# One value product per head, and the division by the row sums moved behind it, in a fused attention and gated-MoE kernel

## The chip, the cores and the metric

The kernel runs on one core of one Trainium2 chip. The metric is device time in microseconds (us) from the first to the last instruction with what lies around it, of one launch; lower is better. The core has TensorE (matmuls; its weight loads are a row of their own, PEld), VectorE (DVE), ScalarE (ACT), GpSimd (POOL) and SyncE (SP), which here issues nearly all transfers.

## The reference

Attention in which a query sees only the keys that fall into its own bucket of a hash, followed by a feed-forward block with a convolution gate. Shapes: batch 4, 8 heads, 768 positions, 64 per head; the feed-forward block is 512 wide. All is float32.

```
mask = bucket(q @ proj)[:, :, :, None] == bucket(k @ proj)[:, :, None, :]   # 6 bits, 64 buckets
scores = where(mask, q @ k.T / sqrt(64), -1e9)
attn = exp(scores - max(scores))
attn = attn / (sum(attn) + 1e-09)
x = concat_heads(attn @ v)                                    # (4, 768, 512)
gate = sigmoid(sum_k conv_w[k] * x shifted by 4 - k)          # 5 taps, causal, per channel
out = (gate * (x @ w_val)) @ w_out
```

## The kernel before, in words

The work is a stream of 32 units (one head of one batch each), and a unit is six tiles of 128 queries. The main loop (line 453) makes one pass per tile, 192 in all; I call such a pass a slot. Everything is issued in program order: `manual_schedule` (line 442) keeps TensorE, ScalarE, VectorE and GpSimd in the order in which the loop calls the helpers. So the order of the calls in the loop is the order on each engine's queue, and an instruction that waits holds all that stand behind it on its engine. SP's queue is not among those engines.

For tile k the stages lie in several slots:
- `scores(k + 1)` (line 225): four matmuls into one of two PSUM tiles `s`. The mask is inside the product: twelve more rows of the operands hold the hash bits, so that keys of other buckets come out hugely negative.
- `maxima`, `factors`, `shifts` (lines 235 to 248) on VectorE: the row maximum from PSUM and two tiny instructions that make scale and bias of the exponential. They depend on each other.
- `exponentials(k)` (line 250) on ScalarE: p = exp(scale * s + bias), with the row sum as a by-product in `sm`.
- `row_sums`, `recip`, `normalise` (lines 260 to 271): for two tiles at a time the reciprocal of the row sum on VectorE, then p times it on GpSimd, for each tile, two slots after its exponential.
- `transposes(k - LAG)` (line 273) with LAG = 3: six 128x128 transposes on TensorE into two PSUM tiles `tp`, at the end of the slot; `keep_transposed` (line 283) copies them to SBUF on ScalarE at the start of the next slot.
- `attn_v` (line 294): the value product, 24 matmul instructions per unit (6 key blocks, two column halves of the array side by side, each product two instructions), into the PSUM tile `av`. It is a generator; the loop steps it twice in every odd slot, 8 instructions each time. At its end ScalarE copies the result to x (line 311).

The rest is generators that the loop steps once or more per slot: `prep` (line 157) builds a coming head's operands, with a cast of the raw q and k on VectorE, the remainder on GpSimd, and seven transfers on SP, all in one step; `bits` (line 186) makes the hash bits of four heads, with a 32-column matmul into a side tile; `pair_x` (line 317) splits x of two heads into a rounded part (VectorE) and a remainder (GpSimd) and runs the five convolution taps on VectorE; after the fourth pair of a batch come the sigmoids, and `cur["gates"]` is 2 for the next two slots, in which the MoE takes three steps; `moe` (line 350) is the feed-forward block in chunks of three steps (four matmuls each) into one PSUM tile from the pool `ps_m`, which has one buffer. `val` ends with the product with the gate, `ht` (line 370), and later its split (`hh`, `hl`); `outp` ends with a copy of the output tile (ScalarE, or VectorE while gates is set, line 394) and its store. `hold` (line 408) keeps two output chunks back until the next batch's MoE begins. `load_weights` splits the weights during the first heads, mostly on VectorE. After the loop (line 490) the MoE has five PSUM tiles and runs alone.

Of the kernel before, what the change touches and what calls it, by code (L numbers as in the profile page):

```python
# [26 lines left out]
def kernel(  # L27
# [18 lines left out]
    LAG = 3  # L46
# [8 lines left out]
    pp = ctx.enter_context(tc.tile_pool(name="pp", bufs=LAG + 1))  # L55
# [7 lines left out]
    op = ctx.enter_context(tc.tile_pool(name="op", bufs=2))  # L63

# [92 lines left out]
    def prep(i):  # L157
# [8 lines left out]
        nc.vector.tensor_copy(out=aq, in_=r)  # L166
# [10 lines left out]
        if j == 3 and i + 1 < len(units):  # L177
            yield
            yield from bits(i + 1)

    def side_tile():
        if not moes:
            return ps_m.tile([P, 512], FP32, name="m")
        return ps_t.tile([P, 512], FP32, name="tp")

    def bits(i):

        u = stk.tile([P, S], FP32R, name="u", bufs=2)
        for hf in range(2):
            yield  # L190
            sl = slice(hf * HS, (hf + 1) * HS)
            z = side_tile()
            for jj in range(4):
# [3 lines left out]
            nc.vector.tensor_scalar(out=u[:, sl], in0=z[:, 0:HS], scalar1=rows_sb[:, 0:1], scalar2=rows_sb[:, 1:2],  # L197
                                    op0=ALU.is_ge, op1=ALU.mult)
        cur["u"] = u

    def first_bits():
        yield from bits(0)
        load_raw(5)
# [46 lines left out]
    def exponentials(k):  # L250
        s, nb = ss.pop(k), nbs.pop(k)
        p = pp.tile([P, 2, HS], FP32, name="p")
        if k % 2 == 0:
            cur["sm"] = small.tile([P, 2, 2], FP32, name="sm")
        sm = cur["sm"]
        nc.scalar.activation(out=p, in_=s[:, :, 0:HS], func=AF.Exp, bias=nb, scale=gs.pop(k), accum_out=sm[:, k % 2, 0:1])  # L256
        ps[k] = (p.rearrange("p a b -> p (a b)"), sm)


    def row_sums(k):  # L260
        sums[k] = small.tile([P, 2, 2], FP32, name="s1")
        nc.vector.tensor_scalar(out=sums[k][:, :, 0], in0=ps[k][1][:, :, 0], scalar1=1e-9, scalar2=None, op0=ALU.add)

    def recip(k):
        ri = small.tile([P, 2], FP32, name="ri")
        nc.vector.reciprocal(out=ri, in_=sums.pop(k)[:, :, 0])
        rcs[k], rcs[k + 1] = ri[:, 0:1], ri[:, 1:2]

    def normalise(k):
        p, _ = ps[k]  # L270
        nc.gpsimd.tensor_scalar(out=p, in0=p, scalar1=rcs.pop(k), scalar2=1.0, op0=ALU.mult, op1=ALU.mult)  # L271

    def transposes(k):
        p, _ = ps.pop(k)
# [19 lines left out]
    def attn_v(i, pts):  # L294
# [4 lines left out]
        for kb in range(KB):  # L299
            if kb:  # L300
                yield
            for s, pt in enumerate(pts):
                nc.tensor.matmul(out=av[s * D:(s + 1) * D, 0:HS], lhsT=vt[:, kb, hh * D:(hh + 1) * D], rhs=pt[kb // 3][:, kb % 3, :],  # L303
                                 start=(kb == 0), stop=(kb == KB - 1), tile_position=(0, s * D))
        if hh == 0:
            x = cur["x"] = xp.tile([P, S + KW - 1], FP32, name="x")
            nc.gpsimd.memset(x[:, 0:KW - 1], 0.0)
        x = cur["x"]
        for s in range(2):
            o = KW - 1 + s * HS  # L310
            nc.scalar.copy(out=x[hh * D:(hh + 1) * D, o:o + HS], in_=av[s * D:(s + 1) * D, 0:HS])  # L311
        if hh == 1:
            if c == 0:
                cur["xs"], cur["g"] = {}, []
            convs.append(pair_x(b, c, x, cur["g"], cur["xs"]))

    def pair_x(b, c, x, gs, xs_):
        for o in (0, HS):
# [4 lines left out]
            nc.vector.tensor_copy(out=xh, in_=x0)  # L323
            nc.gpsimd.tensor_tensor(out=xl, in0=x0, in1=xh.bitcast(FP32), op=ALU.subtract)  # L324
        yield
# [9 lines left out]
        if c == NP - 1:  # L335
# [3 lines left out]
            cur["gates"] = 2  # L339
            moes.append(moe(b, xs_, gs))  # L340

    def acc_tile():
        pools = accs
# [6 lines left out]
    def moe(b, xs_, g):  # L350
# [3 lines left out]
        def later():  # L354
            while todo:
                todo.pop(0)()

        def val(o, j):
# [11 lines left out]
            nc.vector.tensor_tensor(out=ht, in0=acc[:, 0:HS], in1=g[j][:, o:o + HS], op=ALU.mult)  # L370

            def split():
                hh = hp.tile([P, HS], FP32R, name="hh")
                nc.vector.tensor_copy(out=hh, in_=ht)  # L374
# [6 lines left out]
        def outp(o, tb):  # L381
# [4 lines left out]
            for hi, wi in ((0, 0), (0, 1), (1, 0)):  # L386
# [6 lines left out]
                later()  # L393
            ob = op.tile([P, 512], FP32, name="o")
# [4 lines left out]
            r0 = o + tb * P  # L399
# [157 lines left out]
```

## Time and profile before

| | us |
|---|---|
| median of 3 runs | 638.9 |
| lowest, highest | 638.37, 640.07 |
| the profiled execution's own time | 637.56 |
| its span, first to last instruction | 635.6 |
| VectorE busy | 465.9 |
| ScalarE busy | 421.7 |
| GpSimd busy, of which normalise (L271) | 364.7, 220.0 |

The profiled execution's time and its span differ by 2 us, the start and end of the launch. The granted TensorE clock was 0.989 of full speed on average.

How to read the rows: a group's row gives line, engine and operation, what is written and read, the number of instructions, then after the bar their busy time in us and the mean of one in ns, then the idle time of the engine just before them and what ended it. A timeline row gives start in us, duration in us, then the same names; records of one kind that follow each other are merged (x8), and a bracket tells idle time before. Matmuls are pipelined, so their records overlap, and the distance of two starts is the better measure. A row of waits gives total us, times, and the longest. L12 is line 12 of the kernel before, until a kernel after is spoken of.

### The profile page before, as it was taken

The numbers are of one execution on the slowest core, as the hardware profiler recorded it, in microseconds if no ns is written. First come the engines' busy times: TensorE is split into PE (matmuls) and PEld (weight loads), VectorE is DVE, ScalarE is ACT, GpSimd is POOL, SyncE is SP. The second block draws the span as 40 slices with busy tenths as digits, with TensorE's granted clock in tenths as the row PEclk, the third lists the DMA queues.
The fourth block names the chain that finished last, engine by engine and source line by source line (L and its number), as shares of the span: only waits on it lengthen the run. The fifth ranks groups of instructions, "written<-read, shape, count | busy, mean of one in ns | idle before, by whom it ended". The sixth has DMA issues, their size and how long they took to land.

```text
span 635.6 us, 10630 instructions
## 1 busy us (share of the span) xinstructions
PE 590.1 (93%) x3496; PEld 424.3 (67%) x3496; DVE 465.9 (73%) x1064; ACT 421.7 (66%) x881; POOL 364.7 (57%) x326
## 2 busy tenths in 40 slices
PE   4689888878999999999999999999999999999997
PEld 2465554555567777676667877677667777776895
DVE  5789897999986766668675877578685787665532
ACT  3487776767778666667787766677778677675400
POOL 1375868577765764567653776466562677544221
PEclk9899998998999999999999999999999999999999
DMA  6533535443332334343433333343422223300111
GB/s 243 128 101 86 139 96 138 112 134 81 104 80 58 83 75 123 82 105 96 104 80 79 88 80 110 80 121 80 120 57 61 57 53 79 86 18 2 50 51 50
DMA packets 23269, 56.76 MB, mean 89 GB/s; under 512 B 4296, under 2 KB 4296, under 8 KB 23216
## 3 DMA queue, kind: packets, MB, share of 16 engines
q1 hardware_dynamic: 23072, 56.06, 32.9%
q8 instruction: 28, 0.46, 0.3%
q14 instruction: 25, 0.20, 0.1%
q10 hardware_dynamic: 144, 0.03, 0.0%
HBM read 23.12 MB, written 6.29 MB: 46 GB/s over the span
## 4 chain that ended last, share of the span: by engine, by line
PE 64%; DVE 18%; ACT 10%; issue 3%; DMA 3%; POOL 0%; DVEq 0%; ACTq 0%
PE av L303 16%; PE s L232 15%; PE tp L280 12%; PE m L390 8%; PE m L365 7%; DVE nm L238 6%; ACT p L256 4%; DVE g L334 3%; ACT pt L289 3%; ACT x L311 2%; DMA w<-in_w_out_dram 2%; DVE aq L166 1%; PE tp L365 1%; PE tp L390 1%; PE s L390 1%
## 5 line engine op out<-in xcount | busy, mean ns | idle before, releaser
L271 POOL TENSOR_SCALAR p<-p,ri 128x768 f32<-128x768 f32 x192 | 220.0, 1150 | 200.3 <-DVE nb L248 157.6
L256 ACT ACTIVATE p<-s,nb,gs 128x768 f32<-128x768 f32 x192 | 192.7, 1004 | 49.7 <-DVE nb L248 44.6
L289 ACT COPY pt<-tp 128x384 f32<-128x384 f32 x384 | 166.2, 485 | 86.0 <-PE tp L280 85.0
L238 DVE TENSOR_REDUCE nm<-s 128x1 f32<-128x768 f32 x192 | 182.4, 950 | 52.8 <-PE s L232 52.6
L280 PEld LDWEIGHTS tp<-ident,p 128*128 128x128 f32 x1152 | 130.4, 142 | 74.2 <-issue 47.3
L280 PE MATMUL tp<-ident,p 128*128 128x128 f32 x1152 | 165.4, 280 | 4.5 <-ACT pt L289 1.6
L232 PE MATMUL s<-ak,aq 76*128 76x384 f32 x384 | 118.6, 390 | 32.2 <-ACT p L256 25.4
L303 PE MATMUL av<-pt,vt 128*64 128x384 f32 x768 | 146.9, 504 | 0.0
L232 PE MATMUL s<-bk,bq 128*128 128x384 f32 x384 | 101.6, 346 | 0.0
L232 PEld LDWEIGHTS s<-ak,aq 76*128 76x128 f32 x384 | 59.4, 195 | 48.9 <-ACT p L256 39.3
L303 PEld LDWEIGHTS av<-pt,vt 128*64 128x64 f32 x768 | 47.4, 137 | 63.3 <-issue 62.7
L334 DVE SCALAR_TENSOR_TENSOR g<-x,cw_sb,g 128x768 f32<-128x768 f32 x64 | 78.4, 1225 | 0.2
L232 PEld LDWEIGHTS s<-bk,bq 128*128 128x128 f32 x384 | 71.9, 194 | 0.5 <-issue 0.5
L376 POOL TENSOR_TENSOR hl<-ht,hh 128x384 fp32r<-128x384 f32 x32 | 33.4, 1044 | 45.5 <-DVE hh L374 45.5
L168 POOL TENSOR_TENSOR bq<-r,aq 128x768 fp32r<-128x768 f32 x31 | 58.4, 1885 | 0.5 <-DVE aq L166 0.5
L311 ACT COPY x<-av 64x384 f32<-64x384 f32 x64 | 30.4, 475 | 33.5 <-PE av L303 32.9
L365 PE MATMUL m<-xh,wv 128*128 128x384 f32 x200 | 42.7, 337 | 0.0
L248 DVE TENSOR_SCALAR nb<-nm,gs 128x1 f32<-128x1 f32 x192 | 40.1, 209 | 3.5
L370 DVE TENSOR_TENSOR ht<-m,g 128x384 f32<-128x384 f32 x25 | 13.9, 555 | 35.4 <-PE m L365 32.0
L256 ACT ACTIVATION_READ_ACCUMULATOR p<-s,nb,gs 128x1 f32 x192 | 39.1, 204 | 0.0
L324 POOL TENSOR_TENSOR xl<-x,xh 128x384 fp32r<-128x384 f32 x32 | 33.5, 1066 | 9.5 <-DVE xh L323 9.5
L390 PE MATMUL m<-wo,hh 128*128 128x512 f32 x144 | 38.1, 394 | 0.0
(84 smaller groups left out, 475.6 us busy)
## 6 DMA issues: line engine op xcount, KB each, us to landing
r<-in_qk_dram SPq DMA_DIRECT2D x32, 384.0 KB
vt<-in_v_dram SPq DMA_DIRECT2D x16, 384.0 KB
out_dram<-o SPq DMA_DIRECT2D x24, 256.0 KB
ak<-aq SPq DMA_DIRECT2D x31, 192.0 KB
bk<-aq SPq DMA_DIRECT2D x31, 192.0 KB
bk<-bq SPq DMA_DIRECT2D x31, 192.0 KB
bq<-aq SPq DMA_DIRECT2D x31, 192.0 KB
w<-in_w_val_dram SPq DMA_DIRECT2D x4, 512.0 KB
```

What stands on the lines that cost most here:

```text
L168: nc.gpsimd.tensor_tensor(out=bq, in0=r, in1=aq.bitcast(FP32), op=ALU.subtract)
L232: nc.tensor.matmul(out=s[:, hf, 0:HS], lhsT=lq[0:n, qs], rhs=rk[0:n, hf * HS:(hf + 1) * HS], start=n == M, stop=n == P)
L238: nc.vector.tensor_reduce(out=nm, in_=s[:, :, 0:HS], axis=AX.XY, op=ALU.max, negate=True)
L256: nc.scalar.activation(out=p, in_=s[:, :, 0:HS], func=AF.Exp, bias=nb, scale=gs.pop(k), accum_out=sm[:, k % 2, 0:1])
L271: nc.gpsimd.tensor_scalar(out=p, in0=p, scalar1=rcs.pop(k), scalar2=1.0, op0=ALU.mult, op1=ALU.mult)
L280: nc.tensor.transpose(out=tp[:, n * P:(n + 1) * P], in_=p[:, kb * P:(kb + 1) * P], identity=ident)
L289: nc.scalar.copy(out=pt[:, :, qo:qo + P], in_=tp[:, 0:HS].rearrange("p (a b) -> p a b", b=P))
L303: nc.tensor.matmul(out=av[s * D:(s + 1) * D, 0:HS], lhsT=vt[:, kb, hh * D:(hh + 1) * D], rhs=pt[kb // 3][:, kb % 3, :], start=(kb == 0), s ...
L311: nc.scalar.copy(out=x[hh * D:(hh + 1) * D, o:o + HS], in_=av[s * D:(s + 1) * D, 0:HS])
L334: nc.vector.scalar_tensor_tensor(out=g, in0=x[:, k:k + S], scalar=w, in1=g, op0=ALU.mult, op1=ALU.add)
L365: nc.tensor.matmul(out=acc[:, 0:HS], lhsT=wv[wi][:, c, j * P:(j + 1) * P], rhs=xs_[(c, o)][xi], start=(m == 0), stop=(m == 11))
L390: nc.tensor.matmul(out=acc, lhsT=hs[(o, j)][hi][:, tb * P:(tb + 1) * P], rhs=wo[wi][:, j, :], start=(m == 0), stop=(m == 11))
```

## The change

It changes eight things.

1. The value product of a unit is issued whole, in the slot r = 1 of the next unit (`finish(avs)`; r is the slot's place in its unit, 0 to 5). No MoE step is taken in that slot; slot r = 4 takes a second one after its transposes.
2. p is no longer normalised. The row sums of the six tiles of a unit lie in one tile; at r = 0 VectorE takes their reciprocals once per unit, SP writes them to memory, and at r = 1 SP reads them back, spread over 64 partitions twice (`rb`). At r = 3 `take` forms x from `av` on VectorE, as a product with `rb`, whose factors it reads at every third element.
3. LAG is 1: a tile's transposes come one slot after its exponential.
4. Casts move from VectorE to GpSimd: q and k in `prep`, x in `pair_x`, `ht` in the MoE.
5. `prep` begins at r = 5 and spreads its transfers over r = 0, 2 and 3. At the start two steps are taken per slot.
6. The hash bits use the PSUM tile of the value product, at r = 4 and 5.
7. Instructions that read a PSUM tile are put off to the next slot: the bits' comparison and `ht` (list `late`, behind the maximum), and the copy of the output tile with its store (list `puts`, behind the exponential).
8. The convolution takes four steps at r = 2 and one at r = 1; in a batch's last pair and at the end one per slot.

```
@@ prep
-        nc.vector.tensor_copy(out=aq, in_=r)
+        nc.gpsimd.tensor_copy(out=aq, in_=r)
         yield
         nc.gpsimd.tensor_tensor(out=bq, in0=r, in1=aq.bitcast(FP32), op=ALU.subtract)
         nc.sync.dma_start(out=ak[0:D].bitcast(FP32), in_=aq[D:P].bitcast(FP32))
         nc.sync.dma_start(out=bk[0:D].bitcast(FP32), in_=aq[D:P].bitcast(FP32))
+        yield
+        yield
         nc.sync.dma_start(out=bk[D:P].bitcast(FP32), in_=bq[D:P].bitcast(FP32))
+        yield
         nc.sync.dma_start(out=bq[D:P].bitcast(FP32), in_=aq[0:D].bitcast(FP32))
...
@@ bits
-            z = side_tile()
+            z = pool.tile([P, 512], FP32, name=name)
...
-            nc.vector.tensor_scalar(out=u[:, sl], ...
+            late.append(lambda z=z, sl=sl: nc.vector.tensor_scalar(
...
+    def row_sums(i):
+        s1 = small.tile([P, KB], FP32, name="s1", bufs=2)
+        nc.vector.tensor_scalar(out=s1, in0=sms.pop(i), scalar1=1e-9, scalar2=None, op0=ALU.add)
+        ri = small.tile([P, KB], FP32, name="ri", bufs=2)
+        nc.vector.reciprocal(out=ri, in_=s1)
+        rows = dp.tile([2, P, KB // 2], FP32, name="rows")
+        nc.sync.dma_start(out=rows.rearrange("s p t -> p s t"), in_=ri.rearrange("p (s t) -> p s t", s=2))
+        return rows
+
+    def row_factors(i, rows):
+        rb = rbs[i] = rp.tile([P, P, KB // 2], FP32, name="rb")
+        for s in range(2):
+            nc.sync.dma_start(out=rb[s * D:(s + 1) * D], in_=rows[s].partition_broadcast(D))
...
+    def take(i, av):
...
         for s in range(2):
             o = KW - 1 + s * HS
-            nc.scalar.copy(out=x[hh * D:(hh + 1) * D, o:o + HS], in_=av[s * D:(s + 1) * D, 0:HS])
+            nc.vector.tensor_tensor(out=x[hh * D:(hh + 1) * D, o:o + HS].rearrange("d (t p) -> d t p", p=P),
+                                    in0=av[s * D:(s + 1) * D, 0:HS].rearrange("d (t p) -> d t p", p=P),
+                                    in1=rb[s * D:(s + 1) * D].rearrange("d p t -> d t p"), op=ALU.mult)
...
@@ pair_x
-            nc.vector.tensor_copy(out=xh, in_=x0)
+            nc.gpsimd.tensor_copy(out=xh, in_=x0)
             nc.gpsimd.tensor_tensor(out=xl, in0=x0, in1=xh.bitcast(FP32), op=ALU.subtract)
-        yield
...
     def acc_tile():
+        drain(late)
+        drain(puts)
...
@@ val
-            nc.vector.tensor_tensor(out=ht, in0=acc[:, 0:HS], in1=g[j][:, o:o + HS], op=ALU.mult)
+            late.append(lambda: nc.vector.tensor_tensor(out=ht, in0=acc[:, 0:HS], in1=g[j][:, o:o + HS], op=ALU.mult))
...
@@ outp
+            puts.append(lambda: put(o + tb * P, acc))
+            yield
+
+        def put(r0, acc):
             ob = op.tile([P, 512], FP32, name="o")
             if cur["gates"]:
                 nc.vector.tensor_copy(out=ob, in_=acc)
             else:
                 nc.scalar.copy(out=ob, in_=acc)
             nc.sync.dma_start(out=out[b, r0:r0 + P, :], in_=ob)
...
@@ the loop
+            r = k % KB
             if 0 <= k - LAG - 1:
                 keep_transposed(k - LAG - 1)
...
                 maxima(k)
                 factors(k)
                 shifts(k)
+            drain(late)
+            if r == 0 and k:
+                rows = row_sums(tiles[k - 1][0])
+            if r == 1 and k > 1:
+                row_factors(tiles[k - 2][0], rows)
             if k + 1 < N:
...
                 scores(k + 1)
             if k < N:
                 exponentials(k)
-            if k >= 60 or k % 2:
+            drain(puts)
+            whole = bool(avs)
+            for _ in range(1 if whole or k >= N - 10 else 4 if r == 2 else cur["last"]):
                 step(convs)
+            if r == 3:
+                drain(taken)
...
-            for _ in range(3 if cur["gates"] else 1):
+            for _ in range(0 if whole else 3 if cur["gates"] else 1):
                 step(moes)
             cur["gates"] = max(0, cur["gates"] - 1)
             step(preps)
-            if k % 2:
-                step(avs)
-                step(avs)
+            if k < 5:
+                step(preps)
+            if r == KB - 1:
+                finish(preps)
+                preps = [prep(k // KB + 2)]
+                step(preps)
+            finish(avs)
             if 0 <= k - LAG < N:
                 transposes(k - LAG)
+            if r == 4 and not cur["gates"]:
+                step(moes)
```

More of the change, by code (lines that the diff above doesn't have):

```diff
@@ L45 @@
     KW = 5
-    LAG = 3
+    LAG = 1
     scale = 1.0 / float(D) ** 0.5
@@ L178, in prep, with bits @@
             yield
[L179 to L186, printed above, removed]
+            yield from bits(i + 1, ps_v, "av")
+    def bits(i, pool, name):
         u = stk.tile([P, S], FP32R, name="u", bufs=2)
         for hf in range(2):
-            yield
+            if hf:
+                yield
+            drain(late)
             sl = slice(hf * HS, (hf + 1) * HS)
-            z = side_tile()
+            z = pool.tile([P, 512], FP32, name=name)
             for jj in range(4):
@@ L252, in exponentials @@
         p = pp.tile([P, 2, HS], FP32, name="p")
[L253 to L271, printed above, removed]
+        i, qt = tiles[k]
+        if qt == 0:
+            sms[i] = small.tile([P, KB], FP32, name="sm", bufs=2)
+        sm = sms[i]
+        nc.scalar.activation(out=p, in_=s[:, :, 0:HS], func=AF.Exp, bias=nb, scale=gs.pop(k), accum_out=sm[:, qt:qt + 1])
+        ps[k] = p.rearrange("p a b -> p (a b)")
+    def row_sums(i):
[10 more added lines that the diff above has]
+            nc.sync.dma_start(out=rb[s * D:(s + 1) * D], in_=rows[s].partition_broadcast(D))
     def transposes(k):
-        p, _ = ps.pop(k)
+        p = ps.pop(k)
         tps[k] = []
@@ L304, in attn_v @@
                                  start=(kb == 0), stop=(kb == KB - 1), tile_position=(0, s * D))
+        taken.append(lambda: take(i, av))
+    def take(i, av):
+        b, h = units[i]
+        hh, c = h % 2, h // 2
         if hh == 0:
@@ L338, in pair_x @@
                 nc.scalar.activation(out=g, in_=g, func=AF.Sigmoid)
-            cur["gates"] = 2
+            cur["gates"], cur["last"] = 2, False
             moes.append(moe(b, xs_, gs))
     def acc_tile():
+        drain(late)
+        drain(puts)
         pools = accs
@@ L354, in later @@
         def later():
-            while todo:
-                todo.pop(0)()
+            drain(late)
+            drain(todo)
         def val(o, j):
@@ L438, in finish @@
             step(gens)
-    cur["gates"], cur["end"], cur["pts"] = 0, False, []
+    cur["gates"], cur["end"], cur["pts"], cur["last"] = 0, False, [], False
     N = len(tiles)
@@ L496 @@
             step(moes)
-        finish(moes)
+            drain(late)
+            drain(puts)
+        while moes:
+            step(moes)
+            drain(late)
+            drain(puts)
 _INS = ['qk', 'v', 'proj', 'w_val', 'conv_w', 'w_out']
```

42 lines of the change are left out of this document (19 added, 23 removed).

## The prediction

> **What bounds the kernel now.** I read the page's head first, then a table of two windows, then the timeline of TensorE alone, then a stretch of all engines, then the waits.
>
> ```profile
> span 635.6 us, 10630 instructions
> ...
> PE 590.1 (93%) x3496; PEld 424.3 (67%) x3496; DVE 465.9 (73%) x1064; ACT 421.7 (66%) x881; POOL 364.7 (57%) x326
> ```
>
> TensorE is busy 93% of the span, but an average hides stages, so the windows come next.
>
> ```profile
> core 0: us, PE busy (x) PEld busy (x) DVE busy (x) ACT busy (x) POOL busy (x), PEclk, DMA share, GB/s
> 0.00:165.80 165.80, 134.25 (x774) 87.94 (x775) 143.01 (x317) 111.65 (x237) 102.81 (x94) 0.96 0.44 121
> 165.80:635.60 469.80, 455.82 (x2724) 336.34 (x2722) 322.86 (x748) 310.09 (x644) 261.92 (x233) 1.00 0.30 78
> ```
>
> Up to 165.8 us (nine heads; the weights are still being split) VectorE is the busiest, 143 of 165.8 us. Afterwards TensorE is busy 456 of 470 us: whatever shortens TensorE's list there shortens the kernel, and whatever makes it wait is added. So the change has to be priced on TensorE's queue, slot by slot. I call a slot one pass of the main loop (one tile of 128 queries, six per head, r = 0 to 5), S its four score matmuls, T its six transposes, M one step of the MoE (four matmuls). Steady slots:
>
> ```profile
> 415.11 0.86 PE L365 MATMUL m<-xh,wv 128*128 128x384 f32 x4
> 415.90 1.51 PE L303 MATMUL av<-pt,vt 128*64 128x384 f32 x8
> 417.34 0.88 PE L280 MATMUL tp<-ident,p 128*128 128x128 f32 x6
> 417.98 0.59 PE L232 MATMUL s<-ak,aq 76*128 76x384 f32 x2
> ...
> 418.77 0.86 PE L365 MATMUL m<-xh,wv 128*128 128x384 f32 x4
> 419.47 0.82 PE L280 MATMUL tp<-ident,p 128*128 128x128 f32 x6
> 420.04 0.60 PE L232 MATMUL s<-ak,aq 76*128 76x384 f32 x2
> ```
>
> Starts give true pitches, since records overlap. S takes 0.79 (417.98 to 418.77), M of the value projection 0.70, T 0.57 (419.47 to 420.04): 2.06 us for a slot without a value product, with no gap. In a slot with one, M takes 0.79, the eight av matmuls 1.44, T 0.64: the group costs 1.44 + 0.09 + 0.07 = 1.60.
>
> **The change, part by part.**
>
> *1. One value product of 24 matmuls at r = 1 in place of three of 8.* How long is a run of 24? The last head has one already, after the loop:
>
> ```profile
> 585.04 4.39 PE L303 MATMUL av<-pt,vt 128*64 128x384 f32 x24
> 589.36 2.11 PE L390 MATMUL m<-wo,hh 128*128 128x512 f32 x8
> ```
> ```profile
> 585.72 0.15 PEld L303 LDWEIGHTS av<-pt,vt 128*64 128x64 f32 x2 [0.17 <-issue]
> ...
> 588.30 0.15 PEld L303 LDWEIGHTS av<-pt,vt 128*64 128x64 f32 x2 [0.17 <-issue]
> ```
> ```profile
> L256 ACT ACTIVATE p<-s,nb,gs x192: 991/1006/1042, 13.0 to 577.2; 128x768 f32<-128x768 f32 x192
> ```
> ```profile
> 165.80:577.20 411.40, 103.19 (x548) 33.23 (x550) 1.00 0.32 83
> ```
>
> Inside it the pairs follow at (588.30 - 585.72) / 8 = 0.322 us. A group of four pairs is 1.29, so 0.31 of the 1.60 is the price of going into and out of this shape. Twelve pairs in one run: 3.87 + 0.31 = 4.18 against 3 x 1.60 = 4.80, 0.62 saved per head. The run above took 4.32, because its second half started late behind a copy; if each head has that hitch, 0.32 is saved. From 165.8 us to the last exponential 548 av matmuls run (last row), 22.8 heads: **-14.1 us** (bounds -7.3, and -19.2 if the early heads gain too). In front of it stand S and the copies of the transposes, which are done by then, so I take the full value.
>
> *2. The copy of an output tile (`put`) moves from the slot of its last matmul into the next slot, behind that slot's exponential.* This adds a wait: the MoE has one PSUM tile (`ps_m`, one buffer), so the next M cannot start before the copy is done, and T and the next S stand behind that M on TensorE. ScalarE's pace:
>
> ```profile
> 316.68 0.88 PE L280 MATMUL tp<-ident,p 128*128 128x128 f32 x6
> ...
> 317.26 0.86 ACT L289 COPY pt<-tp 128x384 f32<-128x384 f32 x2 [1.23 <-PE tp L280]
> 317.31 0.60 PE L232 MATMUL s<-ak,aq 76*128 76x384 f32 x2
> ...
> 318.01 1.00 ACT L256 ACTIVATE p<-s,nb,gs 128x768 f32<-128x768 f32 x1
> ...
> 318.30 0.96 DVE L238 TENSOR_REDUCE nm<-s 128x1 f32<-128x768 f32 x1 [1.02 <-PE s L232]
> ...
> 318.99 0.87 ACT L289 COPY pt<-tp 128x384 f32<-128x384 f32 x2
> 319.16 0.62 PE L232 MATMUL s<-ak,aq 76*128 76x384 f32 x2 [0.24 <-ACT p L256]
> ...
> 319.61 1.01 DVE L334 SCALAR_TENSOR_TENSOR g<-x,cw_sb,g 128x768 f32<-128x768 f32 x1
> ```
> ```profile
> L370 DVE TENSOR_TENSOR ht<-m,g 128x384 f32<-128x384 f32 x25 | 13.9, 555 | 35.4 <-PE m L365 32.0 <-ACT g L338 3.4
> ...
> L398 ACT COPY o<-m 128x512 f32<-128x512 f32 x12 | 7.0, 587 | 3.2 <-PE m L390 2.2
> ```
>
> From T's start the two copies of T begin after 0.58 (316.68 to 317.26), the exponential 0.75 later, the next ScalarE instruction 0.98 after that: the output copy starts 2.31 us after T and is done at 2.90. T follows the finished M at once; TensorE is back for the next M after T and S, 0.57 + 0.79 = 1.36. It waits 1.54 us with nothing behind to fill in. By the diff's step counts two MoE chunks end per head, at r = 3 and r = 5, and the next chunk begins in the next slot with an M, never with the value product between. Such ends, with ScalarE copying and another chunk right behind: the three tiles of the first half in each of the batches 0 to 2, and the very last tile of batches 0 and 1, behind which the next batch begins. (The first tile of the second half is followed by `hold`, the second is copied by VectorE while `gates` is set, and after the loop there are five PSUM tiles and no deferral.) 11 x 1.54 = **+16.9 us**. If the copy slips in earlier it is 0; it cannot gain, since today's copy holds nobody (M to T has no gap above).
>
> *3. The product with the gate (`ht`) is deferred too, and VectorE gains the division.* From S's start the maximum begins 0.99 later (317.31 to 318.30) and VectorE is free again 1.31 after that (319.61); `ht` takes 0.555, done at 2.86 after S. TensorE's next M is due at 2.06 + 0.79 = 2.85: no wait. But at r = 3 two divisions of 64x384 come first; nearest row `ht`, also one PSUM and one SBUF operand, 0.555 each. The previous maximum's chain ends at -2.06 + 0.99 + 1.31 = 0.24, plus 1.11 is 1.35 instead of 0.99, so M waits 0.37. Nine chunk ends: **+3.3 us** (0 if the division is as fast as its 64 partitions could suggest and fits the gap; see the third rival for the other side).
>
> *4. Slots without an M.* While the MoE holds, TensorE has 1.36 per slot and ScalarE needs 1.73 (317.26 to 318.99), and S waits (0.24 in the row at 319.16). Today every second such slot has a value product, which covers ScalarE; afterwards they come five in a row. Some four more uncovered slots per batch, three batches: 12 x 0.37 = **+4.4 us** (0 to +9).
>
> *5. Waits that go.* With `ht` behind the maximum, exponentials are no longer late, and the side tile of the hash bits no longer takes a transpose's buffer.
>
> ```profile
> PE s L232 <- ACT p L256: 5.1, 15, 0.9
> ...
> PE tp L280 <- DVE u L197: 1.6, 4, 0.4
> ```
>
> **-6.7 us** (0 if all stay).
>
> *6. The first 165.8 us, on VectorE.* Eight heads of it:
>
> ```profile
> L334 DVE SCALAR_TENSOR_TENSOR g<-x,cw_sb,g 128x768 f32<-128x768 f32 x10 | 13.0, 1303 | 0.0
> ...
> L166 DVE CAST aq<-r 128x768 fp32r<-128x768 f32 x8 | 6.0, 755 | 0.0
> ...
> L262 DVE TENSOR_SCALAR s<-sm 128x2 f32<-128x2 f32 x24 | 4.5, 189 | 0.7 <-ACT p L256 0.7
> L266 DVE RECIPROCAL ri<-s 128x2 f32<-128x2 f32 x24 | 4.0, 166 | 0.0
> ...
> L323 DVE CAST xh<-x 128x384 fp32r<-128x384 f32 x6 | 2.6, 471 | 0.0
> ```
>
> Away go the casts, 6.0 + 2.6. In come 16 divisions, 8.9. The row sums look like 8.5 us saved, but they stand today between instructions that wait for each other (maximum, factor, shift), where they cost nothing; once per head at the end of that chain they cost 0.355, 2.8 in all. GpSimd loses the normalisation:
>
> ```profile
> L271 POOL TENSOR_SCALAR p<-p,ri 128x768 f32<-128x768 f32 x192 | 220.0, 1150 | 200.3 <-DVE nb L248 157.6
> ```
>
> With 220 of GpSimd's 365 us gone, the convolution's 1.303 may fall to the 1.01 of the row at 319.61: -2.9. Sum +0.2, **taken as 0**; four convolution steps bunched at r = 2 leave VectorE idle in heads that have none (up to +6), an earlier second `prep` and a quieter GpSimd may give as much.
>
> *The rest costs nothing as long as its cover holds.* GpSimd takes three casts where it gave up 192 normalisations. Scores of the next head need SP's last transfers, issued at r = 3 for r = 5, two slots (4.1 us) ahead. The sums' way through memory:
>
> ```profile
> 40.95 2.29 DMA ak<-u
> ```
> ```profile
> SPq L175 <- PE s L232: 70.7, 15, 7.1
> ```
>
> Two trips of about 2.29 (nearest row) are 4.6 us; between r = 0 and the division at r = 3 lie 1.36 + 5.54 + 2.06 = 9.0. Cover 4.4.
>
> **Sum:** -14.1 + 16.9 + 3.3 + 4.4 - 6.7 + 0 = +3.8. The profiled execution took 637.56 us (span 635.6), so 641.4; the median of the runs shown, 638.9, lies 1.3 above it, so on that scale 642.7: **643 us**. About 0.3% is what a measurement of this kernel can tell from no change.
>
> **The rivals.**
>
> *Faster: the deferred copies hold nobody.* Without the 16.9 of part 2: 626 us. For it: ScalarE is busy only 66%, and a copy that gets in before the exponential in most slots would do. Against: ScalarE works in order, and the copies of T cannot begin before T. It decides from the point where the copy ends within 1.36 of T's start.
>
> *No change: the early part pays.* If VectorE's first 165.8 us are shorter by 5 (quiet GpSimd, earlier second head), 638 us. For it: the 1.303 against 1.01. Against: the bunched convolution.
>
> *Slower: the division is slow.* It reads the factors at every third element. At twice 0.555 it adds 1.11 per head where VectorE paces or delays `ht`: nine early heads and nine chunk ends, +20, 663 us. No row here reads at such a step. [...]
>
> *Slower: the factors come late.* SP works in order; today it stood behind the tiles of `ak` 15 times, 7.1 us at the longest. Past the cover of 4.4 VectorE stops at r = 3 with the next maximum behind it: 15 x 2.7 = 40, 683 us at worst. The transfer that stood there now comes at r = 3, behind these, which speaks against it.
>
> **How the numbers follow.** Forecast 0.46 (with the spread of its terms some of it ends within 0.3% or faster), copies free 0.30, early part pays 0.13, slow division 0.07, late factors 0.04. Faster: 0.30, plus 0.03 of the forecast and 0.03 of the second rival, 0.36. Same: 0.06 of the second rival and 0.07 of the forecast, 0.13. Slower: 0.51. Range 622 to 655: from the first rival with a little more than 14.1 saved, up to the forecast with parts 4 to 6 at their bad ends; the two slow rivals and some of the fringe are left out. The likeliest sign's own range is 641 to 655.
>
> **What would show it.** Right: av in runs of 24 with 4.2 us from start to T; TensorE idle before an M of L365 or L390, released by the output copy on ScalarE, eleven times, some 1.5 us each; ACT and DVE waits of 0.4 at r = 4; VectorE's division near 0.55; its wait for the factors absent. Wrong: no such idle time before M (first rival); a first stage that ends well before 165 us; a division over 0.8 us; VectorE idle until a DMA at r = 3.

## The result: 4.8% slower, and where the time came from

| us | before | after |
|---|---|---|
| median | 638.96 | 669.9 |
| profiled execution, span | 637.56, 635.6 | 671.35, 669.6 |
| heads 1 to 8 | 134.1 | 148.6 |
| heads 9 to 31, to the last exponential | 411.4 | 440.4 |
| TensorE's clock at half in heads 1 to 8; 9 to 31 | 6.8; 0 | 27.3; 10.2 |

The ratio is 1.0476, 95% interval 1.0419 to 1.0534. A stage of heads is counted from the start of its first exponential to the start of the next stage's; the last row adds up the stretches of half speed in the trace's record of TensorE's granted clock, each counted where it begins. A stage's time is that of one profiled execution per kernel, and in the changed kernels the first of heads 1 to 8 alone takes 15.6 to 19.0 us, so two or three us between two stages are no finding. In the fences of this section L12 is a line of the kernel after.

First the page's head and the two windows, cut where the tenth head's first exponential starts (165.8 us before, 178.0 here); their columns are those of the table shown for before.

```profile
span 669.6 us, 10067 instructions
...
PE 588.1 (88%) x3496; PEld 441.0 (66%) x3496; DVE 448.2 (67%) x902; ACT 390.3 (58%) x820; POOL 208.8 (31%) x229
```
```profile
0.00:178.00 178.00, 137.19 (x795) 96.34 (x796) 136.56 (x282) 105.40 (x227) 61.10 (x62) 0.91 0.48 124
178.00:669.60 491.60, 450.95 (x2703) 344.69 (x2701) 311.62 (x621) 284.87 (x593) 147.70 (x168) 0.99 0.34 84
```

Every engine is busy for less time than before (GpSimd 209 us in place of 365), and the kernel is slower: 12.2 us come from the first window, 21.8 from the second. (The 21.8 are 29.0 more up to the last exponential, as in the table, and 7.2 less behind it, 51.2 for 58.4, where 192 matmuls of the MoE are left in place of 212.) In the second TensorE, which sets the time there, is no longer busy 97% but 92%. What it waits for there (total us, times, longest):

```profile
PE s L236 <- ACT p L261: 8.7, 20, 1.7
PE m L407 <- ACT o L419: 8.7, 6, 1.8
PE m L382 <- ACT o L419: 6.6, 5, 1.4
PE m L382 <- DVE ht L387: 6.6, 9, 1.0
PE s L236 <- POOL xl L340: 2.5, 2, 1.3
PE tp L287 <- ACT pt L296: 1.3, 1, 1.3
PE s L236 <- issue: 1.1, 1, 1.1
PE tp L407 <- POOL hh L391: 0.6, 1, 0.6
```
And in the same stage of the kernel before, by its own lines:
```profile
PE s L232 <- ACT p L256: 5.8, 16, 0.9
PE tp L280 <- DVE u L197: 1.6, 4, 0.4
PE tp L280 <- ACT pt L289: 1.0, 2, 0.8
PE s L390 <- DVE hh L374: 0.4, 1, 0.4
```

36.1 us of waits against 8.8, so 27.3 more. Rows two and three are the deferred output copy, row four the deferred product with the gate. The timeline of one deferred copy shows the chain, and something that no row of waits counts:

```profile
231.80 0.81 PE L287 MATMUL tp<-ident,p 128*128 128x128 f32 x6
...
232.80 0.52 PE L236 MATMUL s<-bk,bq 128*128 128x384 f32 x2
...
233.47 0.99 ACT L261 ACTIVATE p<-s,nb,gs 128x768 f32<-128x768 f32 x1 [0.29 <-DVE nb L252]
...
234.45 0.57 ACT L419 COPY o<-m 128x512 f32<-128x512 f32 x1
235.08 1.86 PE L407 MATMUL m<-wo,hh 128*128 128x512 f32 x4 [1.76 <-ACT o L419]
236.73 1.48 PE L287 MATMUL tp<-ident,p 128*128 128x128 f32 x6
```

The next MoE step waits 1.76 us for the copy that stands behind the exponential. After that the six transposes take 1.48 us where the same six took 0.81 ahead of it. The clock column (third from the end) of two windows tells why:

```profile
228.00:233.00 5.00, 5.00 (x32) 4.52 (x31) 4.80 (x9) 4.07 (x10) 0.00 (x0) 1.00 0.60 161
...
235.00:239.30 4.30, 4.22 (x14) 3.50 (x15) 0.00 (x0) 1.55 (x4) 0.74 (x1) 0.60 0.94 245
```

The granted clock was halved for 3.4 us. Three such stretches lie in heads 9 to 31. At half speed 10.2 us do the work of 5.1, so they cost 5.1 where TensorE sets the time.

The first window is another matter: TensorE, VectorE and ScalarE all have idle time there. First the four largest waits of SP's queue from 29.4 to 178 us, then one head's transfers in the timeline:

```profile
SPq L171 <- POOL aq L168: 24.4, 4, 8.7
SPq L180 <- PE tp L287: 16.7, 4, 5.7
SPq L278 <- DMA rows<-ri: 12.4, 7, 3.7
SPq L138 <- POOL x L320: 12.0, 3, 4.1
...
```

The first two are waits of the next head's operands, of a kind that the kernel before has too (28.2, 25.8 and 21.6 us in its three largest rows there); the third is the read of the row sums behind their write, the fourth three loads of weights.

```profile
103.06 0.39 SPq L272 DMA_DIRECT2D rows<-ri  x1
106.32 1.04 POOL L114 TENSOR_TENSOR wv<-w 128x512 fp32r<-128x512 f32 x1
107.30 0.10 POOL L320 MEMSET x<- 128x4 f32 x1
107.39 0.33 SPq L138 DMA_DIRECT2D w<-in_w_out_dram  x1
107.77 0.49 SPq L175 DMA_DIRECT2D bk<-bq  x1
108.35 2.17 SPq L278 DMA_DIRECT2D rb<-rows  x2
...
114.12 1.46 DVE L324 TENSOR_TENSOR x<-av,rb 64x384 f32<-64x384 f32 x2 [1.27 <-DMA rb<-rows]
...
115.61 0.96 DVE L242 TENSOR_REDUCE nm<-s 128x1 f32<-128x768 f32 x1
115.64 0.79 SPq L180 DMA_DIRECT2D ak<-u  x1
...
117.10 0.99 ACT L261 ACTIVATE p<-s,nb,gs 128x768 f32<-128x768 f32 x1 [2.32 <-DVE nb L252]
...
118.28 0.98 PE L236 MATMUL s<-ak,aq 76*128 76x384 f32 x2 [2.57 <-POOL bq L170]
```

SP works in order. At 107.39 it issues a load of weights, held until GpSimd had emptied the staging buffer (the addition at 106.32, L114; the row of waits names the tiny memset behind it); only then come a transfer of the next head's operands and the read of the row sums. So the division waits until 114.12, VectorE's next maximum stands behind it until 115.61, that maximum's exponential until 117.10, and the scores of the next head until 118.28: the exponential frees their PSUM tile at about 118.1. The row names another releaser for these scores, GpSimd's subtraction, which ended at 117.5; the transfer `ak<-u`, issued at 115.64, may have come last too.

### The profile page after: what moved, and what is told of

Its sections match the earlier page's. It is cut to its first block, busy times and chain, and to the rows that moved or that the text cites. A ratio compares the mean times of both kernels' runs of the same rounds, so it can differ in the third digit from the quotient of the medians.

```text
span 669.6 us, 10067 instructions
## 1 busy us (share of the span) xinstructions
PE 588.1 (88%) x3496; PEld 441.0 (66%) x3496; DVE 448.2 (67%) x902; ACT 390.3 (58%) x820; POOL 208.8 (31%) x229
## 4 chain that ended last, share of the span: by engine, by line
PE 50%; DVE 26%; ACT 14%; issue 4%; DMA 4%; POOL 2%; ACTq 0%; DVEq 0%; POOLq 0%; SPq 0%
PE av L310 15%; PE s L236 12%; PE tp L287 10%; DVE nm L242 9%; PE m L382 7%; ACT p L261 7%; PE m L407 5%; DVE x L324 3%; ACT pt L296 3%; DVE g L349 3%; DVE nb L252 2%; DMA rows<-ri 2%; DVE gs L248 2%; ACT g L353 1%; DVE s L268 1%
## 5 line engine op out<-in xcount | busy, mean ns | idle before, releaser
L287 PE MATMUL tp<-ident,p 128*128 128x128 f32 x1152 | 165.8, 281 | 1.3 <-ACT pt L296 1.3
L287 PEld LDWEIGHTS tp<-ident,p 128*128 128x128 f32 x1152 | 138.3, 144 | 39.8 <-issue 23.1
L310 PE MATMUL av<-pt,vt 128*64 128x384 f32 x768 | 132.1, 493 | 0.0
L310 PEld LDWEIGHTS av<-pt,vt 128*64 128x64 f32 x768 | 53.4, 137 | 65.5 <-issue 61.9
L168 POOL CAST aq<-r 128x768 fp32r<-128x768 f32 x31 | 27.1, 876 | 155.8 <-PE s L236 142.1
L349 DVE SCALAR_TENSOR_TENSOR g<-x,cw_sb,g 128x768 f32<-128x768 f32 x64 | 67.8, 1060 | 1.4
L391 POOL CAST hh<-ht 128x384 fp32r<-128x384 f32 x32 | 16.2, 505 | 142.8 <-DVE ht L387 142.8
L382 PE MATMUL m<-xh,wv 128*128 128x384 f32 x208 | 48.9, 361 | 13.2 <-ACT o L419 6.6
L324 DVE TENSOR_TENSOR x<-av,rb 64x384 f32<-64x384 f32 x64 | 42.8, 668 | 15.1 <-DMA rb<-rows 13.7
L382 PEld LDWEIGHTS m<-xh,wv 128*128 128x128 f32 x208 | 36.3, 196 | 19.4 <-DVE ht L387 11.1
L339 POOL CAST xh<-x 128x384 fp32r<-128x384 f32 x32 | 17.9, 560 | 67.6 <-DVE x L324 67.6
```

Of the source, the lines that this page charges most:

```text
L287: nc.tensor.transpose(out=tp[:, n * P:(n + 1) * P], in_=p[:, kb * P:(kb + 1) * P], identity=ident)
L324: nc.vector.tensor_tensor(out=x[hh * D:(hh + 1) * D, o:o + HS].rearrange("d (t p) -> d t p", p=P), in0=av[s * D:(s + 1) * D, 0:HS].rearran ...
L349: nc.vector.scalar_tensor_tensor(out=g, in0=x[:, k:k + S], scalar=w, in1=g, op0=ALU.mult, op1=ALU.add)
L382: nc.tensor.matmul(out=acc[:, 0:HS], lhsT=wv[wi][:, c, j * P:(j + 1) * P], rhs=xs_[(c, o)][xi], start=(m == 0), stop=(m == 11))
```

## The experiments

All are edits of the kernel after unless said otherwise; times are medians, ratios are to the kernel before, which had 637.8 to 639.0 us beside them. The fences of a run have the lines of its own kernel.

**The deferred copy.**
```
-            puts.append(lambda: put(o + tb * P, acc))
+            put(o + tb * P, acc)
```

> The changed kernel with one line put back: the copy of an output tile and its store are issued in the slot of its last matmul again, not in the next slot behind the exponential. Theory (the deferred copy stands in TensorE's way): the changed kernel's 11 idle times before an M that the output copy ended, 15.3 us in all, go, and the median falls from 669.9 to about 655. Rival (the long value product starves the other engines, and the wait for the copy only shows it): the same time is lost at another place, 667 to 672.

649.17 us, 1.0187 (1.0142 to 1.0232): 20.7 us less than the change. The eleven waits were worth 15.3; in heads 9 to 31 the half clock went as well, all 10.2 us of it, and that stage fell from 440.4 to 419.8. 15.3 + 5.1 is 20.4 of these 20.6; the run shows the two together, and the split is worked out from the trace. This kernel is the base of most of what follows; I call it put-now.

**The deferred product with the gate.** On put-now:
```
-            late.append(lambda: nc.vector.tensor_tensor(out=ht, in0=acc[:, 0:HS], in1=g[j][:, o:o + HS], op=ALU.mult))
+            nc.vector.tensor_tensor(out=ht, in0=acc[:, 0:HS], in1=g[j][:, o:o + HS], op=ALU.mult)
```

> The changed kernel with the output copy issued at once (649.2), and the product with the gate too. In the changed kernel M waited for the deferred product nine times, 6.6 us in all. Theory of the prediction (put off, it costs M little, and keeps the exponentials on time): 649 to 656, the waits for M gone and waits of the scores for the exponential grown by more. Rival (it is a deferral like the copy's, and costs what it shows): 642 to 645.

654.15 us, 1.0261 (1.0211 to 1.031), about 5 us slower than put-now, but the two intervals overlap by a little. The trace has what the theory said (165 to 655 us): the waits for the product with the gate fall from 6.6 to 2.3, the scores' waits for the exponential rise from 8.6 to 14.6. So that this deferral pays, in spite of its nine waits, is likely and not shown beyond doubt.

**The convolution.** Of the kernel after:
```
-            for _ in range(1 if whole or k >= N - 10 else 4 if r == 2 else cur["last"]):
-                step(convs)
+            step(convs)
```


> The changed kernel with the convolution stepped once per slot, in place of four times at r = 2 and once at r = 1. Theory (VectorE is overloaded at single slots while the weights are split): heads 3, 5 and 7, which have a convolution and take 20 to 21.5 us where heads 2, 4 and 6 take 16.4 to 17.5, come down by 2 us each, and the first nine heads by 6 to 8; later heads change by less than 3 us in all, so about 662. Rival (these heads are long because SP's queue brings the row sums and the next head's operands late): the first nine heads change by less than 2 us, 667 to 672.

686.03 us, 1.0759 (1.071 to 1.0809): 16 us slower, not faster. Heads 3 and 7 did come down, by 2.3 and 2.5 us, but heads 2, 4 and 6 rose by about 3 each, and heads 9 to 31 took 9.8 more. The idea that the four bunched steps are the early loss fell; that the long product covers them is the likely reason, and not tried.

**SP's queue.** First the kernel after without the row sums' three transfers:
```
-        nc.sync.dma_start(out=rows.rearrange("s p t -> p s t"), in_=ri.rearrange("p (s t) -> p s t", s=2))
...
-            nc.sync.dma_start(out=rb[s * D:(s + 1) * D], in_=rows[s].partition_broadcast(D))
+        rbs[i] = ones_rb
```

> The changed kernel without the way of the row sums through memory: no transfer to it, none back; x is the product with a constant tile, so the output is not divided by the row sums. All instructions of the engines stay, but for these transfers on SP. Theory (SP's queue is late): VectorE's 13.7 us of waiting for the factors go, and with them a part of the 27 us in which a head's first scores wait (8.7 us more than in the kernel before in the first nine heads), so 650 to 658, most of it before 178 us. Rival (the waits are covered by others): 664 or more.

661.15 us, 1.0367 (1.0345 to 1.039): 8.8 less than the change, a little less than expected, with heads 1 to 8 down from 148.6 to 138.6. Then, on put-now, the same transfers issued by GpSimd (`nc.gpsimd.dma_start` in both lines), and in another kernel the weight loads instead:
```
-                nc.sync.dma_start(out=w, in_=src.bitcast(I32).rearrange("p (n t) -> p n t", t=2))
+                nc.gpsimd.dma_start(out=w, in_=src.bitcast(I32).rearrange("p (n t) -> p n t", t=2))
```

> The changed kernel with the output copy issued at once (649.2), and the row sums' three transfers per head issued by GpSimd in place of SP. Theory (SP's queue stands behind the sums: the read waits for the landing of the write, and the next head's operands wait behind it): heads 1 to 8 fall from 146.6 us to about 137, as without the transfers, and the median to about 640. Rival (it is the way through memory itself that comes late, not the queue): heads 1 to 8 stay within 3 us of 146.6.

> The changed kernel with the output copy issued at once (649.2), and the eight weight loads issued by GpSimd, which frees their buffers, in place of SP, where one stood up to 4.1 us for GpSimd with the sums and the operands behind it. Theory (the weight loads hold SP): the long heads 3, 5 and 7 of the first stage (20.95, 19.49, 21.16) lose 2 to 3 us each, about 642. Rival (the sums' own wait holds SP): under 2 us in all.

The sums on GpSimd: 650.32 us, 1.0187 (1.0158 to 1.0217), not the 640 expected and nothing gained; heads 1 to 8 are 5.1 us shorter and the later heads 4.8 longer. The weights on GpSimd: 643.4 us, 1.0083 (1.0055 to 1.0111), heads 1 to 8 down from 146.6 to 139.7, nearly all of it in heads 3, 5 and 7 (21.0, 19.5 and 21.2 us became 18.2, 18.5 and 18.2). Its window of heads 1 to 8:

```profile
29.40:169.10 139.70, 119.43 (x704) 84.97 (x704) 116.98 (x243) 91.78 (x199) 56.45 (x56) 0.93 0.47 118
```

I call this kernel the base. Two controls go with it, by the same two edits: the kernel before with its weight loads on GpSimd, and the base without the sums' transfers.

> The kernel before (639 us) with nothing changed but the queue of the weight loads: GpSimd's in place of SP's. Theory (the change made the weight loads on SP costly, because the row sums' transfers and the spread transfers of the next head now stand behind them with a reader close by; before, SP's waits had cover): no change, 638 to 640. Rival (the weight loads always cost these 7 us on SP, and the changed kernel only shares it): 632.

> The same base (643.4 us) without the transfers of the row sums through memory: x is multiplied by a constant tile and so is not divided by the row sums. Theory (with the weight loads off SP, the 5.6 us that heads 1 to 8 still take longer than before, 139.7 against 134.1, are the sums' three transfers in SP's queue ahead of the next head's operands): heads 1 to 8 fall to about 134 to 135, total 638. Rival (the sums' transfers only mattered behind held weight loads): no change, 642 to 644.

Before with weights on GpSimd: 640.72 us, 1.0038 (1.0022 to 1.0054), no gain, rather a loss of 2.9 us; its heads 1 to 8 take 138.8 in place of 134.1. The base without sums, which leaves the division by them out: 643.21 us, 1.0066 (1.0044 to 1.0088), no change. So the weight loads cost nothing on SP until the row sums stood behind them, and the row sums cost nothing once the weight loads were gone: one loss, the meeting of the two. Moving the loads takes away both their hold on SP and their 512 KB each from its queue; no run separates these two. The third kind of transfer in that queue, the next head's operands, all issued at r = 0, in the base:
```
         nc.sync.dma_start(out=bk[0:D].bitcast(FP32), in_=aq[D:P].bitcast(FP32))
-        yield
-        yield
         nc.sync.dma_start(out=bk[D:P].bitcast(FP32), in_=bq[D:P].bitcast(FP32))
-        yield
...
         load_raw(i + 5)
+        for _ in range(3):
+            yield
```

> The same base (643.4 us) with SP's transfers for the next head not spread: all of them in one slot (r = 0), as the kernel before has them in one step; the hash bits stay at r = 4 and 5. Theory (the spread keeps SP free for the row sums: unspread, SP waits for GpSimd's subtraction, 1.8 us, and for the operands' buffers with the sums behind it): slower by 2 to 6, 645 to 649, mostly in heads 1 to 8. Rival (two slots of lead cover all of it): no change, 643.

653.29 us, 1.0234 (1.02 to 1.0268), 9.9 slower than the base, more than the theory's 2 to 6, and in the profile mostly in heads 9 to 31 (425.6 us against 419.8), not in heads 1 to 8 (142.1 against 139.7). The spread pays, but not where it was thought to.

**What is left of the early loss.** The base still takes 139.7 us for heads 1 to 8 against 134.1. Three kernels: early heads with the product in thirds, the convolution at its old pace and the division at r = 4; the division one slot later in all heads but every fourth; and both:
```
-            for _ in range(1 if whole or k >= N - 10 else 4 if r == 2 else cur["last"]):
+            for _ in range(k % 2 if k < 54 else 1 if whole or k >= N - 10 else 4 if r == 2 else cur["last"]):
...
-            if r == 3:
+            if r == (4 if k < 54 else 3):
                 drain(taken)
...
-            finish(avs)
+            if k >= 54:
+                finish(avs)
+            elif 1 <= r <= 3:
+                step(avs)
+                step(avs)
```
```
-            if r == 3:
+            if r == (3 if k // KB % 4 == 2 else 4):
                 drain(taken)
```

> The same base (643.4 us), but in the first nine heads, while the weights are being split and there is hardly any MoE work, the value product runs in three thirds at r = 1, 2, 3 as in the kernel before, the division at r = 4, and the convolution one step every second slot, not four at r = 2. Theory (with the weight loads off SP, what is left of the loss in heads 1 to 8, 139.7 against 134.1 us, is the bunching: a product of 4.1 us in one slot and four convolution steps in the next, where VectorE and ScalarE pace): these heads fall to about 134 to 136, total 638 to 640. Rival (what is left is the way of the row sums and of the next head's operands through SP's queue, which this does not touch): no change, 643 or a little more for the extra switches, some 2 us.

> The put-now kernel with the weight loads on GpSimd's queue (643.4 us), and the division by the row sums moved from r = 3 to r = 4, behind the product with the gate (it stays at r = 3 in every fourth head, where the hash bits need the same PSUM tile at r = 4). In the trace without this move TensorE waits nine times for that product with the gate, 6.6 us: all at r = 4, right behind the division, 1.01 to 1.05 us three times, 0.66 five times in the heads that keep the division at r = 3, and 0.21 once. Theory (those waits are the division's 1.39 us ahead of the maximum): the three of 1.03 go, -3.1 us, 640.3. Rival (they come from the distance between scores and product with the gate, whatever stands between): no change, 643.4.

> Both of these edits on the same base (643.4 us). Theory: the gains add, about -8, 635 us, faster than the kernel before (639). Rival (neither cause is right): 643 to 645.

Thirds early: 646.95 us, 1.0134 (1.0107 to 1.0161), 142.3 us for these heads; refuted. The division at r = 4: 641.35 us, 1.0053 (1.0035 to 1.007). Its trace has what was meant, and where it went (from head 9 on, 170.6 to 641.5 us; the base, 169.1 to 639.7 us, has 8.2 and 6.6 in these rows):

```profile
PE s L236 <- ACT p L261: 10.1, 18, 1.7
PE m L382 <- DVE ht L387: 3.5, 6, 0.7
```

The waits for the gate fell by the predicted 3.1 and those for the exponential rose by 1.9; all of TensorE's waits there fell from 21.2 to 17.3. But two stretches of half clock, 6.8 us, begin in its heads 9 to 31, where the base has none: some 3.4 us where TensorE sets the time. The stage takes 418.7 us for 419.8, and the intervals of this kernel and the base overlap, so a gain isn't shown. Both: 641.85 us, 1.0058 (1.0038 to 1.0079), not 635. Next, TensorE kept busy with work that nobody reads, in the base and, by six transposes in every even slot, in the kernel before:
```
+                if 6 <= k < 54 and r != 1:
+                    keep_busy(12 if r in (3, 4) and k // KB % 2 else 6)
                 scores(k + 1)
```


> The put-now kernel with the weight loads on GpSimd's queue (643.4 us), with work added that nobody reads: in heads 1 to 8, in the slots without a value product, TensorE transposes the identity six times into the idle MoE tile ahead of the scores (0.57 us at full clock; twelve times at r = 3 and 4 of odd heads, where the scores wait up to 2.0 us). In heads 1 to 8 the profile of the base has TensorE's clock granted at half for 20.5 us, in three stretches of 6.8 us that each begin right after such a wait; the kernel before has 6.8 us there. Theory (what is left of the loss in heads 1 to 8, 139.7 against 134.1, is that half clock: 13.7 us more of it at half speed): the half-clock time falls to about that of the kernel before, the heads to 134 to 136, total 638 to 640. Rival (the half clock is a consequence and off the path, VectorE and ScalarE pace these heads): the same or slower by what the added transposes delay, 643 to 648.

> The kernel before (639 us) with the same added work (six transposes of the identity in every even slot of heads 1 to 8). It has 6.8 us of half clock there, two stretches of 3.4. Theory: at most 3.4 us to gain, 636 to 639. Rival (the added work is on the path in these heads): slower, 640 to 645.

The base: 648.94 us, 1.0165 (1.015 to 1.018). Heads 1 to 8 of it:

```profile
32.20:175.80 143.60, 138.92 (x993) 109.06 (x991) 118.64 (x242) 92.70 (x200) 56.71 (x56) 0.99 0.48 112
```

The clock is 0.99 where it was 0.93 (one stretch of half clock that began at 31.7 us is left), and the heads are not shorter: 3.9 us longer, 3.1 of it in the first of them. But with the added transposes TensorE is busy for 138.9 of the 143.6 us, in the base for 119.4 of 139.7: here it sets the time itself, and what the clock gave back the added work may have taken. So the run doesn't tell whether the half clock costs anything in these heads. The kernel before: 638.91 us, 1.001 (1.0 to 1.002): no gain there from the 6.8 us of half clock that went.

**The whole product alone, and the base without it.** The kernel before with the product in one slot, the same with the copies to x two slots later (issued at r = 5), and the base with its product in thirds, the old pace of the convolution, a MoE step in every slot and the division at r = 4. The last is called the late division alone in what was expected of it, but LAG = 1, the casts on GpSimd, the spread transfers and the deferred product with the gate are in it too:
```
-            if k % 2:
-                step(avs)
-                step(avs)
+            finish(avs)
```
```
-            for _ in range(0 if whole else 3 if cur["gates"] else 1):
+            for _ in range(3 if cur["gates"] else 1):
...
-            finish(avs)
+            if 1 <= r <= 3:
+                step(avs)
+                step(avs)
...
-            if r == 4 and not cur["gates"]:
-                step(moes)
```

> The kernel before with one part of the change alone: the value product of a head is issued whole in the slot r = 3 in which it becomes ready, in place of 8 matmuls in each of three odd slots. All else is as before. Theory (the change of the array's shape costs 0.31 us per group, two groups fewer per head): 638.96 falls by 22.8 x 0.62 = 14 at most, and by 7 if every run starts with the hitch of the last one; 625 to 632. Rival (five slots in a row without cover let ScalarE pace TensorE): no gain, 637 to 645.

> The kernel before with the value product whole at r = 3 as in the run that took 673, and the two copies of its result to x on ScalarE put off to r = 5 of the same head. Theory (there the long product cost because ScalarE, in order, stood 114 us behind it for x): the loss goes and the saving shows, 625 to 635. Rival (a long product in one slot starves the chain of exponentials by itself): 655 or more.

> The late division alone: the put-now kernel with the weight loads on GpSimd's queue (643.4 us), with the value product in three thirds at r = 1, 2, 3 of every head, a MoE step in every slot, the convolution at the pace of the kernel before, and the division at r = 4. Theory (the whole product saves its 14 us of TensorE's list and pays about 4 for slots with nothing to fill and 3 to 6 for products with the gate behind the division): 643 + 14 - 4 - 5 = 648. Rival (bunching the product into one slot without a MoE step, with the convolution behind it, costs as much as it saves; late division alone is what helps): 636 to 640, faster than or the same as the kernel before.

Whole product in the kernel before: 673.15 us, 1.0551 (1.0524 to 1.0577), beyond the theory and the rival; with late copies 689.42 us, 1.0804 (1.0778 to 1.083). I had blamed ScalarE's wait for the product (114 us in the first); in the second it is 4.4, and things got worse, so that theory fell. The second one's TensorE (180 to 655 us) waits for what can't run ahead of a product of four microseconds, the exponential and GpSimd's normalisation:

```profile
PE s L232 <- ACT p L256: 24.1, 43, 1.8
PE tp L280 <- POOL p L271: 12.0, 12, 1.6
PE tp L280 <- ACT pt L289: 5.6, 9, 1.7
```

The base without the whole product: 644.22 us, 1.0088 (1.0071 to 1.0106), 4 us less than expected and the same as the base, 1.0083. TensorE's waits from its head 9 on (172 to 641 us; the base has 8.2 and 6.6 in the two rows, and 21.2 in all against 12.2 here):

```profile
PE s L236 <- ACT p L261: 7.3, 10, 1.5
...
PE m L382 <- DVE ht L387: 0.8, 4, 0.2
```

From this kernel to the base the value products themselves shrink from 99.5 to 92.5 us in heads 9 to 31 (starts of product and next instruction), the scores with what they wait for grow from 110.8 to 117.9: the saving is real and is given back on the spot. The MoE steps, the convolution and the division lie differently in the two as well, so what the whole product does by itself is shown in the kernel before alone.

No version here beats the kernel before; the best, 641.35 us, is 0.5% slower. Which of the parts that all of them share (LAG, the casts, the spread, the deferrals) holds that remainder no run separates.

## Why the prediction was wrong, step by step

Forecast 643, range to 655, time 669.9. The direction was the likeliest one; the size failed in two places. The spans differ by 34.0 us where the sum had 3.8: of the missing 30.2, 12.2 lie in the first window and 18.0 in the second.

*The step that failed first* is part 6 with the sentence behind it, "taken as 0" and "The rest costs nothing as long as its cover holds". The two trips of 2.29 us were compared with 9.0 us of cover as if SP were free in between. (The trip was longer, too: in the rows above the read of the factors is issued by 110.52 us and VectorE goes on, released by it, at 114.12, 3.6 us later.) The last rival had the right mechanism (SP in order, VectorE stopped at r = 3) and was given 0.04, because only the operands' transfer was thought to stand in front. The weight loads, in the same queue, were left out; each is held until a staging buffer is free. VectorE waited for the factors three times there, 7.3 us, and the next head's scores stood too. Weights off SP give back 6.9 of the 14.5 us of heads 1 to 8, and 2.0 went with the output copy put back (1.6 of it in the first of these heads). For the other 5.6 (139.7 against 134.1) no run found the early order of product and convolution, the sums' transfers alone or the spread to be the cause; TensorE's clock stays open. One candidate is the move of the loads itself: by the same edit these heads of the kernel before take 138.8. VectorE's list itself did not grow, as part 6 had it: 116.7 us of work in heads 1 to 8 against 121.9.

*The second window* was to be +3.8 and is +21.8, term by term:

1. Whole product, −14.1. Right: from a run's start to the next instruction's it takes 4.02 us, as from 265.18 to 269.20 here. 69 short runs of 1.44 became 23 of 4.02, 99.5 us became 92.5; the other 7 are the 46 entries and exits less (0.79 for 0.70 us in an M that stands before a product, 0.63 for 0.57 in a T behind one).
```profile
265.18 4.09 PE L310 MATMUL av<-pt,vt 128*64 128x384 f32 x24
269.20 0.87 PE L287 MATMUL tp<-ident,p 128*128 128x128 f32 x6
```
2. Deferred copies, +16.9. Right in mechanism and count: eleven waits, 15.3 us. Short by the halved clock, 5.1, which was not priced; the experiment gives 20.6 for both.
3. Product with the gate, +3.3. Nine waits as counted, 6.6 us: the division takes 0.668 us each in the mean where 0.555 was taken, and two stand ahead of the maximum.
```profile
L324 DVE TENSOR_TENSOR x<-av,rb 64x384 f32<-64x384 f32 x64 | 42.8, 668 | 15.1 <-DMA rb<-rows 13.7
```
4. and 5. Slots without an M, +4.4, and waits that go, −6.7. Part 5 failed. The scores were to wait some 4 us and wait 12.3 (8.7 + 2.5 + 1.1), against 5.8 before. Slots with an M, the slot with the product and, while the MoE holds, slots with neither now follow each other, and where VectorE or ScalarE is one tile behind there is nothing to fill in. This reason is read from the order of the calls, not tried.

In sum −14, +27.3 of waits (forecast: +17.9) and +5.1 of clock make 18.4 of the 21.8; 3.4 I can't place. In the base, without the deferred copies and the half clock, the same stretch (169.1 to 639.7 us) has 12.4 us more of waits than in the kernel before, and takes 470.6 us against 469.8. So the 14 us that the product saves there are nearly all paid back in waits, for which the sum had 1.0.

The rivals: "the copies hold nobody" is refuted by the eleven waits, "the early part pays" by heads 1 to 8. "The division is slow" stands at 0.668 us, a fifth over the unit-step row it was priced by (0.555) and far from the 1.11 of the rival, whose doubling for the step was an assumption that no run shows. The row compared has twice the partitions (128x384 for 64x384), so how much of the fifth is the step's stays open.

## What to carry to other kernels

A transfer's cover is not a distance in slots but the state of its queue: before adding a dependent transfer, list every other one on that in-order queue and what each of them waits for, in every stage. Work that is deferred behind a step of another engine is paid by whoever needs its buffer (here eleven waits of TensorE, 15.3 us), and if TensorE is the one who waits, the wait can be paid a second time as clock (here some 5.1 us). A saving in the switching of one engine's list is worth only as much as the other engines can run ahead over the longer run that makes it: in the kernel before, the whole product alone cost 35 us.

## What was not expected of the hardware

TensorE's clock was halved after as little as 1.6 us of idle time. In the 3.4 us before 235.4 us it was idle 1.76, and 3.4 us of half clock followed. In the traces of the kernel before and the kernel after, eleven such stretches begin between the first and the last exponential; they last 3.4, 6.8 or 10.2 us, and in the 3.4 us ahead of each TensorE has no matmul record for 1.6 to 2.2 us. But a scores wait of 1.74 us in the base's later heads (to 185.2 us) was not followed by one: the granted clock there is 1.00 (165 to 410 us). So what decides is not shown. With the copy put back all three stretches of heads 9 to 31 are gone. The kernel before, whose waits in its later heads are at most 0.9 us, never loses its clock there.

A tiny VectorE instruction lasted as long as the GpSimd instruction beside it: the addition on 128x6 values took 1.39 us, ending with GpSimd's subtraction, where its median is 0.16. In this trace ten of the 32 additions take more than 0.3 us, and each ends 0.03 to 0.07 us behind a GpSimd instruction that began before it. Which of the two holds the other, and by what, no run here tries.

```profile
100.96 1.82 POOL L170 TENSOR_TENSOR bq<-r,aq 128x768 fp32r<-128x768 f32 x1
101.42 1.39 DVE L268 TENSOR_SCALAR s<-sm 128x6 f32<-128x6 f32 x1
```
